# A windowed-attention and two-MLP kernel: the low-word shift of a 64-bit weight moved from VectorE to ScalarE

## The chip, the cores and the metric

The kernel runs on one core of a Trainium2 chip. The metric is the device time of one execution in microseconds; the time before is the median of three runs.

A core has five engines that run their own instruction queues side by side: TensorE (PE, with the weight load PEld beside it), VectorE (DVE), ScalarE (ACT), GpSimd (POOL) and SyncE (SP), which issues the DMAs here. Each engine executes its queue in order, and waits on semaphores of the others.

## The reference, cut to what matters

Three stages follow one another on a batch of 4 x 576 tokens, 8 heads of 64:

```python
x = downsampled_attention(q, k, v) + local_attention(q, k, v)   # window of +-3 positions
h = x @ w_in;  y = (h * cos(h)) @ w_out                         # 512 -> 2048 -> 512
out = ((y @ w_a) * (y @ w_b)) @ w_out2                          # 512 -> 1536 -> 512
```

The five weight matrices come as float64, since they are divided by a NumPy float64 scalar when they are drawn; q, k and v are float32. The chip's engines don't compute in float64, so the kernel turns every 64-bit weight into float32 by its bits: the high word holds sign, exponent and 20 bits of the mantissa, and the top three bits of the low word are the last three that a float32 keeps.

## The kernel before, in words

Weights come as 512 KB blocks, 128 x 512 values of two 32-bit words each, as the tile `raw` (first MLP) or `praw` (second MLP). `to_f32` (L102 to L110) converts a block in three instructions:

- L104, ACT: a Prelu over the high words, taken as float32, scales the exponent into place (in place, every second word).
- L106, DVE: the low words are shifted right by 29, which leaves the top three bits as an integer 0 to 7 (in place).
- L108, DVE: the high word shifted left by 3, OR the low word, gives the float32's bits.

There are 68 blocks. The first 32 belong to the first MLP (`w_in`, `w_out`): `wsplit` (L112 to L117) follows the conversion by an ACT copy to fp32r (`w`, L115) and a POOL subtraction that gives the rest (L116), so that a product of matrices is made of three fp32r products, `mm3` (L419 to L423: hi by hi, hi by lo, lo by hi). The other 36 belong to the second MLP: `pre_conv` (L587 to L603) converts them between the steps of the first MLP, forms sums on POOL (L600 to L603) or a split (ACT L596, POOL L597), and writes them to DRAM, from where the second MLP loads them.

The attention of 8 units of 288 tokens and the first MLP are interleaved. Unit 0 is computed first by itself, then a loop over `g` runs 112 steps: each step makes one block of 128 rows of `h` (`h_mm`), the cosine on ACT and DVE (`cos_a`, `cos_b`, L459 to L468), the split into `gh` (ACT L472) and `gl` (L476, on POOL for the first 8 steps and on DVE afterwards), and, three steps later, the product with `w_out` (`back_mm`). Pieces of the next unit's attention stand between (`unit_slots`): score tiles on DVE (L218 to L223), maxima (L236), an Identity with a per-partition bias on ACT (L237), softmax, transposes and the sums of v on POOL (`vd`, L173 to L175, fed by DMAs into `vs`). The first 32 conversions are asked for by `goal`: about two in a step for 8 steps, then about one in a step. All of them lie in the first 145 us. The last 36 conversions are spread over the time from 207 to 565 us. From 570 us on the second MLP runs alone, and no weight is converted there.

What stands ahead of what on an engine's queue isn't written out by hand alone: a scheduler lays the order down when the program is built, from the order of the source, the dependencies and its own estimates of durations. So the shifts of some blocks stand many steps ahead of the step that asks for them. Loads of raw blocks are paced: a load waits for the conversion (L108) of the block eight before it.

Of the kernel before, what the change touches and what calls it, by code (L numbers as in the profile page):

```python
# [9 lines left out]
F32 = mybir.dt.float32  # L10
# [3 lines left out]
U32 = mybir.dt.uint32  # L14
I64 = mybir.dt.int64
AF = mybir.ActivationFunctionType
ALU = mybir.AluOpType
# [41 lines left out]
def kernel(ctx, tc, qT, kT, vw, vds, w_in, w_out, w_a, w_b, w_out2, out):  # L59
    nc = tc.nc  # L60
    pe, act, dve, pool, sp = nc.tensor, nc.scalar, nc.vector, nc.gpsimd, nc.sync

    const = ctx.enter_context(tc.tile_pool(name="const", bufs=1))
# [28 lines left out]
    def after(ins, earlier):  # L92
        if earlier is not None:
            tc.add_manual_dep(ins.ins, earlier.name,
                              mybir.DependencyInfo(mybir.DependencyClass.NoSync, mybir.DependencyReason.DATA),
                              reason="paces the loads")
# [5 lines left out]
    def to_f32(raw, out=None, behind=None):  # L102
        lw, hh = raw[:, :, 0], raw[:, :, 1]
        ins = act.activation(out=hh.bitcast(F32), in_=hh.bitcast(F32), func=AF.Prelu, scale=2.0 ** -112, alpha=2.0 ** 32)  # L104
        after(ins, behind)
        ins = dve.tensor_scalar(out=lw, in0=lw, scalar1=29, scalar2=None, op0=ALU.logical_shift_right)  # L106
        after(ins, behind)
        ins = dve.scalar_tensor_tensor(out=lw if out is None else out, in0=hh, scalar=3, in1=lw, op0=ALU.logical_shift_left, op1=ALU.bitwise_or)  # L108
        marks.append(ins.ins)
        return lw  # L110

    def wsplit(raw, lo_eng):  # L112
        t = wp.tile([128, 2, 512], F32R, tag="w", name="w", bufs=33)
        lw = to_f32(raw)
        act.activation(out=t[:, 0], in_=lw.bitcast(F32), func=AF.Copy)  # L115
        lo_eng.tensor_tensor(out=t[:, 1], in0=lw.bitcast(F32), in1=t[:, 0].bitcast(F32), op=ALU.subtract)  # L116
        return t[:, 0], t[:, 1]  # L117
# [362 lines left out]
    for a in range(2):  # L480
        r = slice(64 * a, 64 * a + 64)
        pool.affine_select(out=mask[r], in_=mask[r], pattern=[[-1, W]], compare_op=ALU.is_ge,
                           fill=-8e9, base=3, channel_multiplier=1)
        pool.affine_select(out=mask[r], in_=mask[r], pattern=[[1, W]], compare_op=ALU.is_ge,
                           fill=-8e9, base=3, channel_multiplier=-1)

    if C["MK"]:
        identb = const.tile([128, 128], BF16, name="identb")
# [9 lines left out]
    if True:  # L498
# [88 lines left out]
        def pre_conv(n, g):  # L587
            nm, p, j = pre[n]
            t = praw[n]
            hh = t[:, :, 1]  # L590
            flat = t.rearrange("p f e -> p (f e)")
            fb = flat.bitcast(F32)
            k = len(marks)
            to_f32(t, flat[:, :512], h_ins[g])
            if nm == "2":
                act.activation(out=flat[:, 512:].bitcast(F32R), in_=fb[:, :512], func=AF.Copy)  # L596
                pool.tensor_tensor(out=flat[:, :512].bitcast(F32R), in0=fb[:, :512], in1=fb[:, 512:], op=ALU.subtract)  # L597
            else:
                a11, a12, a21, a22, s1, s2, s4 = (fb[:, 128 * i:128 * i + 128] for i in range(7))
                pool.tensor_tensor(out=s1, in0=a21, in1=a22, op=ALU.add)  # L600
                pool.tensor_tensor(out=s2, in0=s1, in1=a11, op=ALU.subtract)
                pool.tensor_tensor(out=a21, in0=a11, in1=a21, op=ALU.subtract)
                pool.tensor_tensor(out=s4, in0=a12, in1=s2, op=ALU.subtract)  # L603
# [113 lines left out]
        for g in range(NG + LAG):  # L717
            if g < NG:
                i, u, f = seq[g]
# [40 lines left out]
        for G in range(len(GROUPS)):  # L760
            for p in range(NP):
                prev = [("back", G, 0, p - 1, i, mh) for i in range(2) for mh in range(2)] if p else []
                a, b = ([("prod", G, p, nm, w) for w in ("P1", "P6", "P2", "P7", "P4", "P5", "P3")] for nm in "ab")
# [125 lines left out]
        for k, it in enumerate(items):  # L889
            stage(k + AH)  # L890
            if it[0] == "prod":
                product(k, *it[1:])
                if it[1] == 0:
                    fetch2(cv[0] + 1)
                    a, b = divmod(np_[0] - 4, 7)
# [3 lines left out]
            else:  # L899
                _, G, h, p, i, mh = it  # L900
                q = 2 * p + i
                if mh == 0 and (h == 1 or p == NP - 1):
                    r = q + 2 if h == 1 else i
                    if r < NF2:
                        f = r // 2 + NP * (r % 2)
# [66 lines left out]
```

## Time and profile before

| | us |
|---|---|
| median of 3 runs | 1010.39 (1010.36 to 1012.73) |
| the profiled execution, its own time | 1010.78 |
| its span, first to last instruction | 1009.0 |
| mean granted TensorE clock over the span | 0.983 |

A profile is one execution. Busy times of an engine are unions: two instructions that overlap in the engine's pipeline count once. Idle time of an engine only matters where it lies on the chain of work that ended last. The clock is the TensorE clock that was granted, as a share of 2.4 GHz.

### The profile page before, as it was taken

To read this page: it belongs to the slowest core of one execution; us is meant where nothing else is said; L and a number is where in the kernel's file an instruction comes from. 1 tells how busy PE (TensorE), PEld (TensorE's weight loads), DVE (VectorE), ACT (ScalarE), POOL (GpSimd) and SP (SyncE) were. 2 spreads that over 40 slices of the span, in tenths; PEclk is the share of its full clock that TensorE was granted. 3 is DMA by queue.
4 is the path that set the end of the run, shared out by engine and by line. 5 is a ranking of instruction groups with operands and counts; after the bars stand their busy time and mean duration, and the time that the engine had idled before them with its cause. 6 is when DMAs were issued, how large, how long until landed. Compare 5 with 4: busy or idle time off the path is not lost.

```text
span 1009.0 us, 18867 instructions
## 1 busy us (share of the span) xinstructions
PE 960.7 (95%) x6936; PEld 915.4 (91%) x6936; DVE 704.1 (70%) x1476; ACT 546.0 (54%) x1258; POOL 344.5 (34%) x463
## 2 busy tenths in 40 slices
PE   5878799999899999999998999999999999999998
PEld 3767789999798989899998999999999999999998
DVE  7788976587577877766466657676677667676751
ACT  4677757566485757566566643443444344434421
POOL 4878751005221341111046235433043330233310
PEclk9969999999899999999999999999999999999999
DMA  9644520153545463432277983316711128634000
GB/s 309 228 154 165 159 65 14 45 169 95 173 127 161 145 169 120 140 102 84 75 228 277 332 275 106 100 62 217 240 35 52 54 77 305 216 132 126 1 32 32
DMA packets 75644, 141.28 MB, mean 140 GB/s; under 512 B 6432, under 2 KB 46624, under 8 KB 75552
## 3 DMA queue, kind: packets, MB, share of 16 engines
q1 hardware_dynamic: 75552, 140.08, 42.2%
q8 instruction: 55, 0.90, 0.4%
q14 instruction: 37, 0.30, 0.1%
HBM read 110.95 MB, written 29.10 MB: 139 GB/s over the span
## 4 chain that ended last, share of the span: by engine, by line
PE 80%; DVE 6%; POOL 5%; DMA 4%; ACT 2%; issue 1%; SPq 1%; POOLq 0%; ACTq 0%; DVEq 0%
PE acc L420 10%; PE acc L421 10%; PE acc L422 10%; PE z L421 9%; PE z L422 9%; PE z L420 9%; PE h L420 6%; PE h L421 5%; PE h L422 5%; DMA vs<-in_vds_dram 2%; PE att L326 2%; PE att L207 1%; DVE raw L108 1%; PE att L319 1%; PE att L234 1%
## 5 line engine op out<-in xcount | busy, mean ns | idle before, releaser
L825 DVE TENSOR_TENSOR ev<-ev,z 128x384 f32<-128x384 f32 x252 | 135.4, 550 | 70.9 <-PE z L422 67.6
L420 PE MATMUL h<-xh,w 128*128 128x288 f32 (+1 forms) x448 | 147.6, 329 | 8.6 <-DVE gs L468 8.5
L420 PE MATMUL acc<-gh,w 128*128 128x288 f32 (+1 forms) x448 | 146.2, 326 | 3.9 <-DVE ev L453 3.9
L422 PE MATMUL h<-xh,w 128*128 128x288 f32 (+1 forms) x448 | 143.1, 319 | 2.2 <-POOL w L116 2.2
L421 PE MATMUL acc<-gl,w 128*128 128x288 f32 (+1 forms) x448 | 142.6, 318 | 2.4 <-POOL gl L476 2.4
L421 PE MATMUL h<-xl,w 128*128 128x288 f32 (+1 forms) x448 | 143.6, 321 | 0.0
L422 PE MATMUL acc<-gh,w 128*128 128x288 f32 (+1 forms) x448 | 141.6, 316 | 0.0
L783 POOL TENSOR_TENSOR sb<-w,sb 128x256 fp32r<-128x256 f32 x96 | 76.1, 794 | 185.9 <-ACT sb L781 140.1
L420 PEld LDWEIGHTS h<-xh,w 128*128 128x128 f32 x448 | 86.5, 193 | 15.3 <-DVE gs L468 12.1
L421 PE MATMUL z<-xl,sb 128*128 128x384 f32 x288 | 97.0, 337 | 0.0
L420 PE MATMUL acc<-gh,wb 128*128 128x384 f32 x288 | 96.9, 337 | 0.0
L422 PE MATMUL acc<-gh,wb 128*128 128x384 f32 x288 | 96.9, 337 | 0.0
L422 PE MATMUL z<-xh,sb 128*128 128x384 f32 x288 | 96.9, 336 | 0.0
L420 PE MATMUL z<-xh,sb 128*128 128x384 f32 x288 | 96.9, 336 | 0.0
L421 PE MATMUL acc<-gl,wb 128*128 128x384 f32 x288 | 96.9, 336 | 0.0
L781 ACT ACTIVATE sb<-w 128x256 fp32r<-128x256 f32 x144 | 59.9, 417 | 66.2 <-PE z L422 63.1
L420 PEld LDWEIGHTS acc<-gh,w 128*128 128x128 f32 x448 | 85.1, 190 | 10.6 <-DVE ev L453 5.0
L783 POOL TENSOR_TENSOR sb<-ws,sb 128x256 fp32r<-128x256 f32 x72 | 54.5, 757 | 108.6 <-ACT sb L781 84.8
L422 PEld LDWEIGHTS h<-xh,w 128*128 128x128 f32 x448 | 86.6, 193 | 4.5 <-POOL w L116 2.4
L421 PEld LDWEIGHTS acc<-gl,w 128*128 128x128 f32 x448 | 85.3, 191 | 4.2 <-POOL gl L476 2.7
L421 PEld LDWEIGHTS h<-xl,w 128*128 128x128 f32 x448 | 86.6, 193 | 1.6 <-issue 0.6
L422 PEld LDWEIGHTS acc<-gh,w 128*128 128x128 f32 x448 | 85.3, 190 | 1.4 <-issue 0.4
(135 smaller groups left out, 2280.4 us busy)
## 6 DMA issues: line engine op xcount, KB each, us to landing
wb<-wd SPq DMA_DIRECT2D x72, 512.0 KB
raw<-in_w_in_dram SPq DMA_DIRECT2D x16, 512.0 KB
raw<-in_w_out_dram SPq DMA_DIRECT2D x16, 512.0 KB
praw<-in_w_a_dram SPq DMA_DIRECT2D x12, 512.0 KB
praw<-in_w_b_dram SPq DMA_DIRECT2D x12, 512.0 KB
praw<-in_w_out_dram SPq DMA_DIRECT2D x12, 512.0 KB
wd<-praw SPq DMA_DIRECT2D x12, 512.0 KB
wd_a<-praw SPq DMA_DIRECT2D x12, 448.0 KB
```

The source lines that it names most:

```text
L108: ins = dve.scalar_tensor_tensor(out=lw if out is None else out, in0=hh, scalar=3, in1=lw, op0=ALU.logical_shift_left, op1=ALU.bitwise_or)
L207: pe.matmul(p[r, W * w:W * w + W], qt[u, hp][r, off:off + W], kt[b, hp][r, BASE[half] + off:BASE[half] + off + W], start=not pem, stop=True,)
L234: pe.matmul(p[a][:QD, :SD], qd[u, hp][r, :], kd[b, hp][r, :], start=True, stop=True)
L319: pe.matmul(p[64 * a:64 * a + 64, NB:NB + QD], vdt[b, hp][:, a, c], pd[u, hp][:, 2 * a + c], start=(c == 0), stop=(c == 1),)
L326: pe.matmul(p[64 * a:64 * a + 64, xo:xo + n], vt[u, hp // 2][r, w, a], pt[u, hp // 2][r, w, 64 * a + qo:64 * a + qo + n], start=True, stop ...
L420: i = pe.matmul(ps_out, lh, rh, start=start, stop=False)
L421: pe.matmul(ps_out, lh, rl, start=False, stop=False)
L422: pe.matmul(ps_out, ll, rh, start=False, stop=stop)
L781: act.activation(out=t[:, 0], in_=blk, func=AF.Copy)
L783: (dve if nst[0] % C["SD"] == 0 else pool).tensor_tensor(out=t[:, 1], in0=blk, in1=t[:, 0].bitcast(F32), op=ALU.subtract)
L825: dve.tensor_tensor(out=dst, in0=a, in1=z, op=ALU.add)
```

## The change

The DVE shift is replaced by an ACT Identity. It reads byte 3 of the low word (the top byte, an unsigned 8-bit integer, one in every 8 bytes), multiplies it by 1/32, adds a per-partition bias `down`, and writes the result as a 32-bit unsigned integer over the low word. The whole part of byte/32 is the same 0 to 7 that the shift gave. Whether the conversion to an integer rounds or cuts off is found out on the chip: 0.75 is converted once at the start; where this gives 1 the bias is -31/64, so that rounding leaves the whole part, and where it gives 0 the bias is 0. That adds a DVE memset, an ACT copy and a DVE multiplication on a 128 x 1 tile ahead of everything else. The dependencies of the two other instructions stay; the OR of L108 now waits for ACT alone.

```diff
         ins = act.activation(out=hh.bitcast(F32), in_=hh.bitcast(F32), func=AF.Prelu, scale=2.0 ** -112, alpha=2.0 ** 32)
         after(ins, behind)
-        ins = dve.tensor_scalar(out=lw, in0=lw, scalar1=29, scalar2=None, op0=ALU.logical_shift_right)
+        top = raw.rearrange("p f e -> p (f e)").bitcast(mybir.dt.uint8).rearrange("p (f b) -> p f b", b=8)[:, :, 3]
+        ins = act.activation(out=lw, in_=top, func=AF.Identity, scale=1.0 / 32.0, bias=down[:, :1])
         after(ins, behind)
         ins = dve.scalar_tensor_tensor(out=lw if out is None else out, in0=hh, scalar=3, in1=lw, op0=ALU.logical_shift_left, op1=ALU.bitwise_or)
...
+
+    down = const.tile([128, 1], F32, name="down")
+    near = const.tile([128, 1], U32, name="near")
+    dve.memset(down, 0.75)
+    act.activation(out=near, in_=down, func=AF.Copy)
+    dve.tensor_scalar(out=down, in0=near, scalar1=-31.0 / 64.0, scalar2=None, op0=ALU.mult)
```

## Rows read from the trace of the kernel before

**Rows 1.** The page: busy time, share and instruction count of each engine

```profile
PE 960.7 (95%) x6936; PEld 915.4 (91%) x6936; DVE 704.1 (70%) x1476; ACT 546.0 (54%) x1258; POOL 344.5 (34%) x463
```

**Rows 2.** By stretch: length; busy (count) PE, PEld, DVE, ACT, POOL; PEclk, DMA, GB/s

```profile
0.00:37.00 37.00, 23.77 (x238) 18.75 (x239) 26.39 (x67) 18.01 (x51) 21.48 (x40) 1.00 0.81 285
37.00:70.00 33.00, 25.04 (x234) 19.46 (x233) 31.48 (x68) 24.51 (x62) 23.67 (x23) 0.84 0.53 182
70.00:115.00 45.00, 38.41 (x288) 36.33 (x287) 38.11 (x56) 34.28 (x80) 34.27 (x30) 0.89 0.55 184
115.00:145.00 30.00, 26.45 (x239) 24.01 (x238) 24.81 (x47) 18.86 (x44) 20.71 (x25) 0.94 0.18 55
...
207.00:540.00 333.00, 327.42 (x2781) 303.14 (x2778) 234.01 (x562) 215.74 (x488) 91.56 (x150) 0.99 0.46 144
540.00:570.00 30.00, 26.82 (x130) 25.27 (x129) 23.24 (x38) 19.59 (x39) 14.57 (x21) 0.94 0.76 248
```

**Rows 3.** Chain that ended last, shares by line: 37-70, 70-115 and 115-145 us

```profile
by line: DVE raw L106 14.2%; DVE raw L108 10.6%; PE att L326 7.3%; DVE smx L223 6.8%; PE att L207 6.1%; DVE smd L293 5.4%; DVE sl L275 4.7%; PE att L319 4.3%; DVE mxd L236 4.0%; DVE smx L218 3.9%; ACT L464 3.9%; DVE mx L222 3.6%; PE h L421 
...
by line: DVE raw L108 24.7%; DVE raw L106 12.4%; PE h L420 7.1%; DVE gl L476 6.7%; PE h L422 6.2%; PE h L421 6.1%; ACT w L115 5.3%; PE att L326 3.7%; ACT raw L104 2.8%; POOL w L116 2.7%; DVE gs L468 2.6%; DVE gs L460 2.4%; issue 2.4%; PE at
...
by line: POOL w L116 23.9%; DMA vs<-in_vds_dram 23.7%; issue 11.8%; POOL vd L174 10.7%; POOL vd L173 9.9%; POOL vd L175 9.6%; ACT w L115 6.8%; ACT smd L237 1.8%; DVE gs L468 1.6%; ACT gh L472 1.5%; ACT gs L467 1.1%; ACT gs L464 1.1%; DVE gl
```

**Rows 4.** L106 by tile: min/median/max ns, first and last start

```profile
L106 DVE TENSOR_SCALAR raw<-raw x32: 399/667/1549, 6.4 to 117.9; 128x512 uint32<-128x512 uint32 x32
...
L106 DVE TENSOR_SCALAR praw<-praw x36: 404/422/1003, 216.8 to 562.4; 128x512 uint32<-128x512 uint32 x36
```

**Rows 5.** L106 alone by stretch: DVE busy time (count)

```profile
37.00:70.00 33.00, 6.51 (x9) 0.84 0.53 182
70.00:115.00 45.00, 11.69 (x14) 0.89 0.55 184
...
207.00:540.00 333.00, 14.79 (x31) 0.99 0.46 144
```

**Rows 6.** Timeline around 55 us: start, duration, engine, line, operation

```profile
54.31 1.28 DVE L108 SCALAR_TENSOR_TENSOR raw<-raw 128x512 uint32<-128x512 uint32 x2
...
54.63 3.49 POOL L476 TENSOR_TENSOR gl<-gs,gh 128x288 fp32r<-128x288 f32 x1 [1.75 <-ACT gh L472]
...
55.51 0.75 DVE L106 TENSOR_SCALAR raw<-raw 128x512 uint32<-128x512 uint32 x2
```

**Rows 7.** ACT groups by form: busy us, mean ns; idle before, releaser

```profile
L104 ACT ACTIVATE praw<-praw 128x512 f32<-128x512 f32 x36 | 23.9, 664 | 4.9 <-DMA praw<-in_w_out_dram 4.9
L237 ACT ACTIVATE smd<-att,mxd 72x144 f32<-72x144 f32 x64 | 22.5, 370 | 19.3 <-DVE mxd L236 19.1
...
L311 ACT COPY smd<-att 72x288 f32<-72x288 f32 x32 | 12.4, 389 | 2.3 <-PE att L309 1.2 <-DVE sd L288 1.0
...
L596 ACT ACTIVATE praw<-praw 128x512 fp32r<-128x512 f32 x12 | 7.6, 631 | 0.8 <-DVE praw L108 0.4
...
L336 ACT COPY up<-att 128x72 f32<-128x72 f32 x32 | 6.9, 216 | 15.3 <-PE att L326 15.1
```

**Rows 8.** ACT timeline at 107 us, two Prelu conversions back to back

```profile
107.44 1.23 ACT L104 ACTIVATE raw<-raw 128x512 f32<-128x512 f32 x2
```

**Rows 9.** L104 alone by stretch: ACT busy time (count)

```profile
37.00:70.00 33.00, 2.89 (x5) 0.84 0.53 182
70.00:115.00 45.00, 9.39 (x14) 0.89 0.55 184
...
207.00:540.00 333.00, 20.58 (x31) 0.99 0.46 144
```

**Rows 10.** Waits of TensorE in 207-540 us: total, times, longest

```profile
PE att L207 <- ACT praw L596: 3.8, 1, 3.8
```

**Rows 11.** ACT timeline of the first 7 us

```profile
0.73 1.28 ACT L237 ACT_TABLE_LOAD   x1 [0.73 <-PEq L958]
6.50 0.38 ACT L237 ACTIVATE smd<-att,mxd 72x144 f32<-72x144 f32 x1 [4.48 <-DVE mxd L236]
```

## The prediction

> **What bounds the kernel now.** I read the page's busy times first: TensorE is busy 95% of the span, DVE 70%, ACT 54% [rows 1]. That is an average, so the next view is the table by stretch, cut where conversions begin and end [rows 2]. From 207 to 540 us TensorE is busy 327.4 of 333 us: only 5.6 us are there to be won. From 37 to 145 us, where the first 32 weight blocks are converted, TensorE is busy 25.0 of 33, 38.4 of 45 and 26.4 of 30 us, so 18 us are idle, and the granted clock is 0.84, 0.89 and 0.94. If the missing shares are stretches at the lower of the two levels, 1.2 GHz, they mean another 33 x 0.16 = 5.3, 45 x 0.11 = 5.0 and 30 x 0.06 = 1.8 us of clock. In the stretch from 37 to 70 us DVE is busy 31.5 of 33 us: it is the bound. From 70 to 115 us TensorE and DVE stand at 38.4 and 38.1, and ACT and POOL at 34.3 each.
>
> The third view is the chain that ended last in the same stretches [rows 3]. From 37 to 70 us the shift L106 leads it with 14.2% (4.7 us); from 70 to 115 us the OR L108 leads with 24.7% and L106 follows with 12.4% (5.6 us). From 115 to 145 us the chain is POOL's subtraction of weights and the v sums with their DMAs; L106 doesn't show.
>
> **What is removed.** 68 shifts leave DVE. Undisturbed one takes 0.40 us, the least of both tiles; the first 32 have a median of 0.667 and go up to 1.549, the last 36 a median of 0.422 [rows 4]. By stretch that is 6.5 us in 37 to 70 (9 shifts), 11.7 in 70 to 115 (14), and 14.8 in 207 to 540 (31) [rows 5]. What is above 0.40 is not work. Around 55 us two ORs, two shifts and further ORs run on DVE without a gap, and a POOL subtraction over 288 columns that began among them takes 3.49 us [rows 6]: the two engines hold each other up when both work from SBUF. Such a hold goes to the next DVE instruction when the shift is gone, so I count a shift as 0.40 us, and its full time as the far end: 3.6 to 6.5 us in 37 to 70, 5.6 to 11.7 in 70 to 115.
>
> **What is added.** 68 Identities on ACT. No row shows one that reads bytes. The nearest is the Prelu L104 on the same blocks with the same stride of 8 bytes, 0.664 us; a copy of the same length that lies dense takes 0.631 (L596) [rows 7], so the stride matters little. The bias from a tile has its price: L237, an Identity with such a bias over 144 columns from PSUM, takes 0.370 us, while copies from PSUM without one take 0.216 over 72 columns and 0.389 over 288 [rows 7], which puts 144 at 0.274. That is 0.096 more, so I take 0.664 + 0.096 = 0.76 us; the ends are 0.63 (dense, no bias) and twice L104, 1.33. Back to back, two L104 take 1.23 us [rows 8], so the second adds 0.57; an Identity then adds 0.57 + 0.10 = 0.67 us to ACT (ends 0.53 and 1.24).
>
> The Trainium skill (ScalarE: Activation LUTs, What ACT_TABLE_LOAD costs) gives 280 ns plus 0.833 ns an element for an activation with such a bias, 0.71 us for 512 columns. By that figure the tight stretch below would have 14 x 0.05 = 0.7 us less on ACT; the sum goes by the rows.
>
> As many Identities as Prelu operations fall in a stretch, so the counts are those of L104: 5, 14 and 31 [rows 9]. ACT's busy time becomes 24.5 + 5 x 0.67 = 27.9 of 33 us, and 34.3 + 14 x 0.67 = 43.7 of 45 us, while DVE falls to 31.5 - 3.6 = 27.9 and 38.1 - 5.6 = 32.5. So the first stretch is relieved and in the second ACT takes over DVE's place.
>
> **The new wait.** L108 waits for ACT alone now. On ACT's queue the Identity stands ahead of the weight copy L115 and of the cosine's and split's operations (L459 to L472); DVE's L460 and L468, POOL's L116 and, three steps later, TensorE wait for those.
>
> **The start.** The three setup operations go ahead of ACT's and DVE's first work. ACT loads its table at 0.73 us and then sits idle 4.48 us before its first operation at 6.50 [rows 11]; that idle time hides one copy, and even one more table load of 1.28 us. Without that cover it would cost at most 1.5 us. The dependency of the bias on DVE is long met when the first Identity needs it. No DMA is added, and the queues of SP and POOL lose nothing and gain nothing.
>
> **The sum, stretch by stretch.**
> - 0 to 37 us: POOL's sums of v wait for DMAs here; one hold of POOL by a shift goes. I take -0.4 (ends 0 and -1.5).
> - 37 to 70 us: 9 x 0.40 = 3.6 us of DVE's work leave a stretch that DVE bounds; one Identity in five I let fall on the chain, 0.67. That is -2.9 (ends: the chain's whole share of L106, -4.7, and all five Identities on the chain with nothing won, +3.4).
> - 70 to 115 us: 5.6 us leave DVE, 9.4 come to ACT, which still fits in 45 us with 1.3 to spare. I take 0 (ends -5.6 and +6.4, the latter worked out below).
> - 115 to 145 us: the chain is POOL's and the DMAs'. 0 (ends -1 and +2).
> - 207 to 540 us: 31 x 0.67 = 21 us come to ACT, which goes from 215.7 to 236.5 of 333 us, and 31 x 0.40 = 12 us leave DVE. TensorE's work hides both. Only where TensorE waits behind the conversions of a block already, 3.8 us once [rows 10], do I add one Identity: +0.7 (ends 0 and +3). If that cover is gone, an Identity ahead of the cosine costs 0.67 each time.
> - 540 to 570 us: five conversions, shift against Identity: 0 (ends -0.6 and +2).
> - Clock: with about a third of the idle time in 37 to 70 us gone, I take back a fifth of its 5.3 us: -1.1 (ends 0 and -2.6).
>
> Together -0.4 - 2.9 + 0 + 0 + 0.7 + 0 - 1.1 = -3.7 us against the profiled execution's 1010.78, or 1007.1. That execution lies 0.39 above the median of the runs, so the forecast is 1006.7 against 1010.39.
>
> **The rivals.**
> - *The large gain.* All of L106's share of the chain goes, 4.7 + 5.6 = 10.3 us, and half of the first stretch's clock comes back, 2.6: 1010.39 - 12.9 = 997.5. For it: DVE saturated in the first stretch. Against it: ACT at 43.7 of 45 us in the second.
> - *Hidden.* The holds between POOL and DVE pass to L108, whose place on the chain is the larger, and ACT's new work eats what is left: 1010, between 1008 and 1012. For it: L108 with 24.7% of the chain stands right behind the shift.
> - *ACT becomes the bound.* From 70 to 115 us the busiest engine got 38.4 of 45 us, 85%. If ACT gets no more either, its 43.7 us need 51.4: +6.4; with two Identities ahead of TensorE's waits in 207 to 540 us, +1.3, and nothing won before 70 us: 1018.1. It decides if ACT keeps more than 1.3 us of idle time in the 45. For it: the copy, the cosine and the split share ACT's queue with the conversion; against it: POOL and DVE, on which ACT waits, are freed. The Trainium skill (ScalarE: Activation LUTs, Rules for kernel authors) speaks for this side: simple arithmetic belongs on VectorE, which is faster for each element. Here a shift has 0.40 us at best on DVE, and the nearest ACT operation 0.664 [rows 4, 7], so by that rule the time would be this rival's, 1018.
> - *It doesn't do what it says.* Each Identity calls for a table load of 1.28 us. L237 is an Identity too, 64 times [rows 7], and the load at 0.73 us is the only one on its line [rows 11]. I give it 0.02.
>
> **How the numbers follow.** 0.3% of 1010.39 is 3.0 us, about what can be told from no change here. The forecast has 0.43, with a range of its own from 1003.5 to 1009; some 0.28 of it lies below 1007.4 and 0.15 above. The large gain has 0.15, hidden 0.18, ACT as the bound 0.22 and the table loads 0.02; these two end slower, but for 0.03 of the first, which stays within 0.3%. So faster 0.28 + 0.15 = 0.43, same 0.15 + 0.18 + 0.03 = 0.36, slower 0.21. The order on the queues is laid down anew when durations change, which no row shows; I let it widen the range to 997 to 1017, which leaves out about a third of the large gain and half of the slow cases, under 0.2.
>
> **What would show it.** Right: from 37 to 70 us DVE is no longer full and TensorE's idle time falls from 8 us to about 5; an Identity takes about 0.76 us; ACT is the busiest engine for the weights after 70 us; the time past 145 us is unchanged to within 1 us. Wrong: ACT idle more than 1.3 us in that stretch with TensorE waiting for the cosine or for weights; Identities far above 0.76 us; L108 longer than before by what the shift gave up; or a wait for ACT at TensorE in 207 to 540 us that sums to more than 3 us.

## The result and the profile after

The changed kernel takes 1001.69 us (median of four runs, 999.70 to 1003.24) against 1010.79 us (1010.36 to 1012.73) for the kernel before; the ratio is 0.988 with a 95% interval of 0.985 to 0.991. It is 1.2% faster, 9.1 us between the medians, more than twice the forecast of 3.7 us. The profiled execution took 1003.24 us, 7.5 less than that of before, with a span of 1001.5 us.

The busy times of the page after, to be laid beside [rows 1]:

```profile
PE 964.9 (96%) x6936; PEld 917.0 (92%) x6936; DVE 669.1 (67%) x1410; ACT 581.9 (58%) x1327; POOL 327.9 (33%) x463
```

DVE has 35.0 us less, ACT 35.9 more, POOL 16.6 less, though the change gives POOL nothing to do or to leave. The table by stretch, cut as in [rows 2] (columns: stretch, length, busy time and count of PE, PEld, DVE, ACT and POOL, PEclk, DMA share, GB/s):

```profile
0.00:37.00 37.00, 22.62 (x238) 17.88 (x239) 22.98 (x61) 20.39 (x55) 19.14 (x39) 0.71 0.84 285
37.00:70.00 33.00, 31.30 (x175) 24.50 (x175) 22.31 (x51) 22.67 (x56) 16.39 (x19) 0.55 0.45 150
70.00:115.00 45.00, 39.88 (x393) 37.08 (x393) 32.15 (x58) 41.74 (x95) 32.49 (x34) 0.92 0.57 179
115.00:145.00 30.00, 28.69 (x223) 26.78 (x223) 21.35 (x43) 26.86 (x65) 17.80 (x24) 1.00 0.36 123
145.00:207.00 62.00, 59.32 (x572) 54.95 (x571) 41.85 (x99) 40.13 (x95) 10.73 (x10) 1.00 0.19 58
207.00:540.00 333.00, 325.68 (x2765) 300.65 (x2764) 224.91 (x528) 233.41 (x521) 90.05 (x155) 1.00 0.46 143
540.00:570.00 30.00, 29.43 (x142) 28.09 (x143) 17.49 (x30) 22.13 (x42) 10.39 (x15) 0.94 0.85 288
```

From 70 to 115 us DVE falls from 38.1 to 32.2 and ACT rises from 34.3 to 41.7, much as forecast, and yet TensorE is busier than before, 39.9 for 38.4, and in the 30 us after that 28.7 for 26.4. ACT has 3.3 us of idle time in the 45, not the 1.3 of the forecast, for the work that falls into a stretch isn't the same. A fixed stretch of time is a poor ruler when the work moves; a fixed piece of work is a better one. I take the steps `g` of the first MLP, and as a step's mark the first ACT operation of the cosine, of which there are 112, one a step. Step 4 and step 20, first before and then after (the timeline of ACT: start, duration, line, operation):

```profile
74.56 0.41 ACT L459 ACTIVATE gs<-h 128x288 int32<-128x288 f32 x1 [0.56 <-PE h L422]
...
152.03 0.39 ACT L459 ACTIVATE gs<-h 128x288 int32<-128x288 f32 x1
```

```profile
77.35 0.41 ACT L460 ACTIVATE gs<-h 128x288 int32<-128x288 f32 x1
...
146.32 0.40 ACT L460 ACTIVATE gs<-h 128x288 int32<-128x288 f32 x1
```

From step 4 to step 20 the kernel before takes 77.5 us, the changed one 69.0: 8.5 us are won there, where the blocks from about the 14th on are converted. The same piece of work in the columns of the table above, before and then after:

```profile
74.56:152.03 77.47, 64.98 (x533) 60.23 (x531) 65.54 (x108) 53.78 (x124) 52.58 (x53) 0.94 0.39 127
```

```profile
77.35:146.32 68.97, 63.02 (x541) 58.72 (x539) 49.26 (x92) 62.99 (x142) 46.30 (x52) 0.98 0.49 161
```

DVE has 16.3 us less to do in it and ACT 9.2 more; ACT is now as busy there as TensorE. From step 20 to the end another 1.8 us are won (855.2 for 857.0). Up to step 4 the changed execution is 2.8 us late, and its clock was low there, as its table in tens shows:

```profile
10.00:20.00 10.00, 5.57 (x59) 3.86 (x55) 9.58 (x26) 7.82 (x20) 2.14 (x5) 0.77 0.88 248
20.00:30.00 10.00, 6.93 (x69) 5.47 (x70) 7.75 (x24) 4.77 (x19) 9.29 (x14) 0.50 1.02 357
...
50.00:60.00 10.00, 10.00 (x48) 6.92 (x49) 3.54 (x11) 6.40 (x15) 4.34 (x6) 0.50 0.73 241
60.00:70.00 10.00, 8.30 (x40) 7.80 (x41) 9.93 (x24) 8.75 (x26) 5.00 (x4) 0.67 0.23 92
```

From about 15 to past 60 us TensorE was granted 0.50, the lower of its levels, after it had been busy 3.6 us of the first ten; the kernel before, with 4.2 there and 5.7 in the next ten, was granted 1.00 and had its low between 60 and 77 us. Not every execution of the changed kernel has it: another one, profiled later (run e12 below), had a mean clock of 0.991 in place of 0.969 and a span of 994.6 us, with step 4 at 73.3 and step 20 at 142.1 us. A low clock need not cost that time: e1's execution below was granted 0.50 from 15 to 46 us and reached step 4 at 73.5.

The parts that were priced one by one:

```profile
L107 ACT ACTIVATE praw<-praw,down 128x512 uint32<-128x512 uint8 x36 | 27.1, 753 | 0.0
L107 ACT ACTIVATE raw<-raw,down 128x512 uint32<-128x512 uint8 x32 | 24.2, 757 | 0.1
...
L104 ACT ACTIVATE raw<-raw 128x512 f32<-128x512 f32 x32 | 21.5, 673 | 0.7 <-DMA raw<-in_w_in_dram 0.7
```

An Identity takes 757 and 753 ns; 0.76 us had been taken. At the start (timeline of ACT) the table load and the one copy stand in idle time, and the first real operation comes 0.07 us later than before:

```profile
0.73 1.28 ACT L491 ACT_TABLE_LOAD   x1 [0.73 <-PEq L965]
2.02 0.20 ACT L491 ACTIVATE near<-down 128x1 uint32<-128x1 f32 x1
6.57 0.38 ACT L238 ACTIVATE smd<-att,mxd 72x144 f32<-72x144 f32 x1 [4.34 <-DVE mxd L237]
```

What came unforeseen is the OR, here before and then after (groups of DVE by form: count, busy us, mean ns, idle before, releaser):

```profile
L108 DVE SCALAR_TENSOR_TENSOR raw<-raw 128x512 uint32<-128x512 uint32 x32 | 31.1, 983 | 1.5 <-ACT raw L104 1.3
```

```profile
L109 DVE SCALAR_TENSOR_TENSOR raw<-raw 128x512 uint32<-128x512 uint32 x32 | 26.1, 819 | 9.4 <-ACT raw L107 9.2
```

The OR itself, untouched by the change, went from 983 to 819 ns. The missing shift alone doesn't explain that: in e4 below, which has no shift either, the OR takes 984 ns. With the shift (24.6 us for the first 32, the mean of 783 ns that the group has) DVE spent 55.7 us on these blocks and now spends 26.1: 29.6 us have gone, more than the far end of the forecast, which was the shift's full time. Elsewhere DVE lost some of it again: three other groups grew by 7.5 us together (by the line numbers of the kernel before: L293 from 16.1 to 19.5, L476 over 288 columns from 39.0 to 41.4, L223 from 17.7 to 19.4).

In 207 to 540 us the 3.8 us that TensorE waited behind a conversion [rows 10] are gone; the longest waits there in this execution are:

```profile
PE h L421 <- DVE gs L469: 1.4, 3, 0.7
PE att L208 <- DVE smx L219: 1.2, 1, 1.2
```

### The profile page after: what moved, and what is told of

Its sections match the earlier page's. It is cut to its first block, busy times and chain, and to the rows that moved or that the text cites. A ratio compares the mean times of both kernels' runs of the same rounds, so it can differ in the third digit from the quotient of the medians.

```text
span 1001.5 us, 18883 instructions
## 1 busy us (share of the span) xinstructions
PE 964.9 (96%) x6936; PEld 917.0 (92%) x6936; DVE 669.1 (67%) x1410; ACT 581.9 (58%) x1327; POOL 327.9 (33%) x463
## 5 line engine op out<-in xcount | busy, mean ns | idle before, releaser
L423 PE MATMUL acc<-gh,w 128*128 128x288 f32 (+1 forms) x448 | 142.1, 317 | 0.0
L421 PEld LDWEIGHTS acc<-gh,w 128*128 128x128 f32 x448 | 84.8, 190 | 9.1 <-issue 2.9
L469 DVE SCALAR_TENSOR_TENSOR gs<-gs,h 128x288 f32<-128x288 f32 (+1 forms) x112 | 55.2, 493 | 56.6 <-ACT gs L468 56.3
```

The source lines that it names most:

```text
L421: i = pe.matmul(ps_out, lh, rh, start=start, stop=False)
L423: pe.matmul(ps_out, ll, rh, start=False, stop=stop)
L469: dve.scalar_tensor_tensor(out=s, in0=s, scalar=1.0, in1=hps[g], op0=ALU.subtract, op1=ALU.mult, reverse0=True)
```

## The experiments

Twelve runs were made, each timed against the kernel before. The ratios are from all executions. Steps 4 and 20 are from the one that was profiled, and one execution can differ from the next by some us: the two of the changed kernel are 4 us apart at step 4, and e7's is the slowest of its ten (1011.6 us, median 1007.35).

| run | shift of blocks 1-13, 14-32, last 36 | ratio to before, 95% interval | step 4, us | step 20, us | 4 to 20 |
|---|---|---|---|---|---|
| before | DVE, DVE, DVE | | 74.6 | 152.0 | 77.5 |
| e3, setup alone | DVE, DVE, DVE | 0.9988 (0.9969 to 1.0008) | 80.0 | 153.2 | 73.2 |
| e9, shift in two pieces | DVE, DVE, DVE | 0.9988 (0.9968 to 1.0009) | 78.0 | 153.3 | 75.2 |
| e2, last 36 | DVE, DVE, ACT | 0.9962 (0.9944 to 0.9980) | 81.5 | 155.3 | 73.8 |
| e10, early 13 | ACT, DVE, DVE | 0.9996 (0.9973 to 1.0018) | 74.1 | 151.7 | 77.6 |
| e7, late 19 | DVE, ACT, DVE | 0.9940 (0.9912 to 0.9968) | 81.1 | 151.1 | 70.0 |
| e1, first 32 | ACT, ACT, DVE | 0.9866 (0.9842 to 0.9891) | 73.5 | 142.6 | 69.1 |
| changed kernel | ACT, ACT, ACT | 0.9880 (0.9854 to 0.9906) | 77.3 | 146.3 | 69.0 |
| e12, changed again | ACT, ACT, ACT | 0.9881 (0.9845 to 0.9916) | 73.3 | 142.1 | 68.8 |
| e8, constant bias | ACT, ACT, ACT | 0.9879 (0.9837 to 0.9920) | 74.9 | 144.7 | 69.7 |
| e11, constant bias | ACT, ACT, DVE | 0.9938 (0.9914 to 0.9961) | 74.4 | 145.1 | 70.7 |
| e4, no low word | none | 0.9887 (0.9851 to 0.9922) | 74.4 | 146.2 | 71.8 |
| e5, extra held operation | ACT and DVE, ACT and DVE, ACT | 0.9960 (0.9940 to 0.9980) | 79.5 | 151.2 | 71.7 |
| e6, extra free operation | ACT, ACT, ACT | 0.9896 (0.9846 to 0.9946) | 75.2 | 145.2 | 70.0 |

The edits are shortened. Those of e1, e2, e5, e6 and e8 are shown against the changed kernel, those of e4 and e9 against the kernel before, those of e7 and e10 against e1.

**Which blocks carry it: e1, e2, and the order by itself: e3.**

```diff
-        ins = act.activation(out=lw, in_=top, func=AF.Identity, scale=1.0 / 32.0, bias=down[:, :1])
+        if out is None:    # e1; e2 has "is not None"
+            ins = act.activation(out=lw, in_=top, func=AF.Identity, scale=1.0 / 32.0, bias=down[:, :1])
+        else:
+            ins = dve.tensor_scalar(out=lw, in0=lw, scalar1=29, scalar2=None, op0=ALU.logical_shift_right)
```

e3 is the kernel before with the five lines of the setup and nothing else.

> Identity on ACT for the 32 blocks of the first MLP only; the other 36 keep the shift on DVE. If the gain is DVE relieved while the first 32 blocks are converted (theory A), this keeps nearly all of it: 0.989 to 0.994 of before, about 1002 us. If the gain comes from the queues being laid down in another order (theory B), the time has no reason to stand near either kernel: anything from 0.985 to 1.005. If it came from the last 36 blocks, 0.998 to 1.002.

> Identity on ACT for the last 36 blocks only; the first 32 keep the shift. Theory A: only the one wait of TensorE near 262 us can go, so 0.996 to 1.001 of before, 1006 to 1011 us. Theory B: anything from 0.985 to 1.005. If the last 36 carry the gain: 0.990 or less.

> The shift stays on DVE for all 68 blocks; only the three setup operations are added and their result is not used. Theory A: 0.998 to 1.002 of before. Theory B: the order on the queues changes here too, so a move of several us, 0.3% or more to either side, speaks for it.

e1 keeps the whole gain, e2 has a third of it, and e3 none. Theory A (the gain is DVE relieved while the first 32 blocks are converted) holds against theory B (another order on the queues): the first 32 blocks carry the gain, and the other order that e3 has doesn't bring it. The last 36 have their own small share: in e1, where they keep the shift, TensorE's wait behind a block's conversion (at 262 us in the kernel before, at 254 in e1) is there as in [rows 10] (waits of TensorE in 207 to 540 us):

```profile
PE h L420 <- DVE gs L468: 4.1, 3, 3.4
PE att L207 <- ACT praw L596: 3.7, 1, 3.7
```

The second line is gone in the changed kernel and in e12. Between step 34 and step 46 the kernels with Identity for these blocks gain 3.6 to 4.4 us on the kernel before (e12: 201.6 to 256.2, before: 210.7 to 268.9, so 3.6), and e1 gains 0.4. Much of it is lost again later: from step 46 to the last step e2 takes 314.5 us and the kernel before 311.1. e2 ends with 0.4%.

**Is ACT's work hidden: e4.** The low word is left out of the weights altogether; the OR takes zeros.

```diff
-        ins = dve.tensor_scalar(out=lw, in0=lw, scalar1=29, scalar2=None, op0=ALU.logical_shift_right)
-        after(ins, behind)
-        ins = dve.scalar_tensor_tensor(..., in0=hh, scalar=3, in1=lw, ...)
+        ins = dve.scalar_tensor_tensor(..., in0=hh, scalar=3, in1=zero[:, :1].to_broadcast([128, 512]), ...)
```

> Leaves out the low word altogether: neither shift nor Identity, the OR takes a zero from a 128 x 1 tile, so a float32 weight lacks its last three mantissa bits. Neither DVE nor ACT has the work. Theory A: at least as fast as the changed kernel, 0.980 to 0.988 of before, 990 to 999 us, since ACT is relieved too; if the 0.76 us of the Identity is wholly hidden on ACT, the same as the changed kernel, 0.988. Theory B: again anything, also slower than the changed kernel.

The same as the changed kernel. In the tight stretches ACT has 4 and 8 us less than in the changed kernel, and TensorE gets no more:

```profile
70.00:115.00 45.00, 39.54 (x312) 36.87 (x309) 33.33 (x48) 37.54 (x87) 35.29 (x33) 0.95 0.61 202
115.00:145.00 30.00, 26.45 (x237) 23.78 (x236) 24.22 (x48) 18.66 (x46) 18.09 (x24) 0.94 0.24 70
```

That doesn't yet show that the Identity is free, for e4 changes the OR too. With `zero` as its second operand the OR of the first 32 blocks is as long as in the kernel before, and POOL is busy 338.1 us against 327.9 in the changed kernel:

```profile
L108 DVE SCALAR_TENSOR_TENSOR raw<-raw,zero 128x512 uint32<-128x512 uint32 x32 | 31.2, 984 | 7.3 <-ACT raw L104 6.8
```

What ACT gave may have gone there. e8 below takes a smaller piece from ACT and leaves the OR's operands alone.

**DVE's time or its holding: e5, e6.** Both are the changed kernel with one more DVE operation on the dead high words of the first 32 blocks, after the OR, whose result nobody reads.

```diff
         marks.append(ins.ins)
+        if out is None:
+            dve.tensor_scalar(out=hh, in0=hh, scalar1=29, scalar2=None, op0=ALU.logical_shift_right)            # e5
+            dve.tensor_reduce(out=hh[:, :1].bitcast(F32), in_=hh[:, :248].bitcast(F32), axis=AX.X, op=ALU.max)  # e6, in its place
```

> The changed kernel, with one more shift of 128 x 512 words on DVE for each of the first 32 blocks, after the OR, on the dead high words, whose result nobody reads: DVE has the time back (0.40 us undisturbed, as the shift removed), ACT keeps the Identity. If DVE's time is what was won (theory A), most of the gain goes: 0.995 to 1.005 of before. If the gain was that the OR and what follows no longer stand behind the shift, as a matter of dependency and not of DVE's time (rival), it stays near 0.988.

> As the run with the extra shift, but the extra DVE operation is a maximum over 248 columns of the dead words, about 0.40 us, of a kind that the trace shows with no lengthening while POOL works (the sums of L180 take 0.44 and 0.74 us throughout). The queues are the same on PE, POOL and SP as with the extra shift. If DVE's own 0.40 us is the price (A1): the same as with the extra shift within 0.3%. If the shift's price is that it and POOL hold each other up (A2): this one is faster than the extra shift by 0.4% or more, 0.988 to 0.993 of before.

The extra operation of e5 in its views by tile (min/median/max) and by form (count, busy us, mean ns):

```profile
L109 DVE TENSOR_SCALAR raw<-raw x32: 411/420/1840, 20.6 to 168.2; 128x512 uint32<-128x512 uint32 x32
```

```profile
L109 DVE TENSOR_SCALAR raw<-raw 128x512 uint32<-128x512 uint32 x32 | 19.5, 608 | 0.2
```

The same for e6:

```profile
L109 DVE TENSOR_REDUCE raw<-raw x32: 393/401/416, 20.5 to 162.1; 128x1 f32<-128x248 f32 x32
```

```profile
L109 DVE TENSOR_REDUCE raw<-raw 128x1 f32<-128x248 f32 x32 | 12.9, 402 | 0.2
```

Both take 0.40 to 0.42 us undisturbed. The maximum never takes more than 0.416 and costs next to nothing, 0.9896 against 0.9880, well inside the intervals. The shift goes up to 1.84 us, has a mean of 0.608, and gives back two thirds of the gain.

The pair is close. In the two traces the queues of TensorE and POOL have the same order, and those of DVE and ACT differ by a few neighbours that change places between 107 and 114 us. Step 4 comes well before that, and 4.3 of the 7.5 us between the two executions are there already (the medians are 6.2 apart): with the same order, an extra operation of the same undisturbed length costs more when it is the shift. The busy times of the two pages, e5 and then e6:

```profile
PE 963.5 (96%) x6936; PEld 914.9 (91%) x6936; DVE 686.5 (68%) x1442; ACT 584.0 (58%) x1327; POOL 335.1 (33%) x463
```

```profile
PE 959.6 (96%) x6936; PEld 913.1 (91%) x6936; DVE 682.0 (68%) x1442; ACT 582.7 (58%) x1327; POOL 328.8 (33%) x463
```

DVE is busy 4.5 us longer with the shift and POOL 6.3 us longer, though POOL's 463 instructions are the same: the hold lengthens both engines. Up to step 4 it is POOL alone, 45.0 us against 41.5, with DVE at 53.8 and 53.9 and a mean clock of 0.89 and 0.91. So the loss there isn't DVE's own time, and the subtraction of 3.49 us among DVE's shifts and ORs [rows 6] fits. Which of POOL's operations carries the loss to TensorE wasn't traced. The rival of a pure dependency falls: nothing depends on the extra shift.

**Early or late: e7, e10.**

```diff
-        if out is None:
+        if out is None and len(marks) >= 13:    # e7; e10 has "< 13"
```

> Identity for the blocks 14 to 32 of the first MLP only (those converted after about 70 us in the trace of before); the first 13 and the last 36 keep the shift. If the gain arises while ACT, DVE and POOL convert one or two blocks in each step after 70 us, as the two traces show, this keeps it: 0.986 to 0.991 of before. If it arises before 70 us, where my prediction put it, 0.996 to 1.001.

> Identity for the first 13 blocks only (converted before about 70 us); the other 55 keep the shift. The counterpart of the run with blocks 14 to 32, which kept half of the gain. If the halves add up: 0.991 to 0.995 of before. If what is won before 70 us is lost at the next bound: 0.997 to 1.002, and then the run with blocks 14 to 32 fell short by its start alone.

The halves don't add up, 0.994 and 1.000 against 0.987 for both, and the columns of steps 4 and 20 suggest why. With late blocks on ACT, step 20 follows step 4 by 68.8 to 70.7 us, in all seven kernels that have it without an extra shift. With late blocks on DVE step 20 comes between 151.7 and 155.3 us in all five, however early step 4 was (74.1 to 81.5). So before, the start is waited away: my reading is that DVE with its shifts can't have the late blocks ready sooner. Blocks 1 to 13 bear on when step 4 comes: 73.3 to 75.2 us with Identity, Copy or no low word, 77.3 in the one with the long low clock, 78.0 to 81.5 with shifts or with e5's extra shift, except for the kernel before itself, with 74.6. Part of that spread may be the clock, though e1 came at 73.5 with a mean of 0.70: up to step 4 its mean was 0.83 or 0.84 in e2, e7 and e9, 0.90 in the kernel before and e3, 0.91 in e10 and e12. In its profiled execution e7 has the fast run from step 4 on but begins it at 81.1, and e10 begins at 74.1 and is held up after that. By the ratios both are needed for all of the gain.

**Meant as a shift that POOL can't hold up: e9.**

```diff
-        ins = dve.tensor_scalar(out=lw, in0=lw, scalar1=29, scalar2=None, op0=ALU.logical_shift_right)
+        cut = 511 if out is None else 512
+        ins = dve.tensor_scalar(out=lw[:, :cut], in0=lw[:, :cut], scalar1=29, ...)
+        if out is None: after(dve.tensor_scalar(out=lw[:, cut:], in0=lw[:, cut:], scalar1=29, ...), behind)
```

> The kernel before, with the shift of the first 32 blocks on DVE in two pieces, 511 words and one word. The Trainium skill (VectorE: DVE Perf Modes, What auto-detection actually checks) has an operation with one SBUF source run at two elements a cycle only where the length is even or the same on both sides; no run here has shown that yet. If the piece of 511 then takes more than 0.5 us, and no longer stretches while POOL works, the holding goes and DVE's own time rises, to some 0.65 to 0.75 us a block. If the holding alone is the price of the shift: 0.988 to 0.994 of before. If DVE's whole time is, held or not: 0.997 to 1.003, since 0.7 us stands against a mean of 0.78 before. If the length changes nothing: 1.000 to 1.005, one more operation.

```profile
L106 DVE TENSOR_SCALAR raw<-raw x32: 404/614/3229, 6.7 to 121.8; 128x511 uint32<-128x511 uint32 x32
...
L107 DVE TENSOR_SCALAR raw<-raw x32: 122/141/147, 7.0 to 125.2; 128x1 uint32<-128x1 uint32 x32
L109 DVE SCALAR_TENSOR_TENSOR raw<-raw x32: 676/868/2198, 8.4 to 140.7; 128x512 uint32<-128x512 uint32 x32
```

The piece of 511 words still takes 0.404 us at the least and is held up to 3.2 us. The test was badly chosen: the length was odd but the same on both sides. For that the Trainium skill (VectorE: DVE Perf Modes, What auto-detection actually checks) still gives two elements a cycle, and the run agrees with it, 0.404 us for 511 words against 0.399 for 512 [rows 4]. A shift on DVE that isn't held has not been tried. What is left is that one more DVE operation of 0.14 us a block, 4.5 us in all, cost nothing that can be measured.

**Cheaper on ACT: e8, e11, e12.** In e8 a Copy with the constant bias -31/64 takes the place of the Identity with the bias tile, and the setup goes; e11 does so for the first 32 blocks and leaves the last 36 on DVE; e12 is the changed kernel again. The constant takes for granted that the conversion to an integer rounds, which no time here can show.

```diff
-        ins = act.activation(out=lw, in_=top, func=AF.Identity, scale=1.0 / 32.0, bias=down[:, :1])
+        ins = act.activation(out=lw, in_=top, func=AF.Copy, scale=1.0 / 32.0, bias=-31.0 / 64.0)
```

> The changed kernel with the bias -31/64 as a constant of a Copy, without the setup operations and the bias tile: each conversion 0.66 to 0.67 us in place of 0.76, 0.09 x 32 = 3 us less on ACT in the first 145 us. If ACT bounds that stretch now: 0.984 to 0.987 of before. If ACT's time is hidden, as leaving out the low word suggests: 0.987 to 0.990, the same as the changed kernel.

> The two cheapest parts together: a Copy with the constant bias for the first 32 blocks, the shift on DVE for the last 36, no setup. If ACT has slack wherever it converts, the same as the changed kernel within 0.3%: 0.985 to 0.990 of before. If ACT's 0.76 us in the first 145 us or the 21 us in 207 to 540 us cost anything: 0.980 to 0.985.

> The changed kernel again, on the same chip as the run with the two cheapest parts, so that the two can be compared: 0.986 to 0.991 of before.

The Copy has a median of 672 ns for the 757 of the Identity (e8, by tile):

```profile
L106 ACT ACTIVATE raw<-raw x32: 650/672/753, 7.6 to 151.9; 128x512 uint32<-128x512 uint8 x32
```

The 0.085 us a block, 2.7 us for the first 32, are worth nothing that can be measured. e11 was expected beside e1 and e8 and is 0.6 to 0.7% behind them, with the interval of e1 clear of its own. Up to step 20 it is within 0.4 us of e8; then it loses, 2.9 us by step 34. Its stretches from 145 us on, and after them those of e1:

```profile
145.00:207.00 62.00, 58.38 (x547) 54.91 (x546) 38.92 (x93) 37.11 (x89) 9.56 (x9) 0.94 0.17 53
207.00:540.00 333.00, 328.02 (x2778) 304.10 (x2777) 233.89 (x559) 215.58 (x487) 93.77 (x152) 0.99 0.45 143
```

```profile
145.00:207.00 62.00, 59.85 (x577) 55.36 (x577) 41.57 (x102) 38.94 (x95) 8.52 (x8) 1.00 0.21 66
207.00:540.00 333.00, 323.57 (x2741) 299.68 (x2741) 233.32 (x555) 215.47 (x485) 97.13 (x159) 0.99 0.45 142
```

From 145 to 207 us e11 has a clock of 0.94, which stood at 0.83 from 150 to 170 us; e1's is 1.00. TensorE had been busy 8.6 and 8.5 of 10 us in the two slices before; in e8, which kept 1.00, it had been busy 7.7 and 8.2, so these shares don't explain it. And from 207 us on it keeps the wait that the shift for the last 36 leaves:

```profile
PE att L207 <- ACT gs L467: 3.8, 1, 3.8
```

e11 differs from e1 in the Copy, the setup and the order that the scheduler laid down with them. That the order is what cost the 0.6% and brought on the clock is likely, but wasn't shown; the cause stays open. No version beat the changed kernel clear of the intervals: e1, e8 and e12 are all within 0.2% of it.

## Why the prediction was right, and where its sum was off

The direction, the range (997 to 1017) and the price of the parts held: an Identity 0.76 us, the start for nothing, ACT nearly full after 70 us. That the time fell inside the range is in part luck: the range had been widened for a new order on the queues, and the gain came from a stretch that the sum had at 0. The size was off, 3.7 us forecast against 9.1 between the medians, and it was off in named terms.

- *0 to 37 us, -0.4, and 37 to 70 us, -2.9.* Step 4 comes 2.8 us later in the profiled execution and 1.3 us earlier in e12. The place was wrong: DVE was full there, and Identity for those blocks alone (e10) wins nothing by the end.
- *70 to 115 us, 0, and 115 to 145 us, 0.* This is the term that was mis-sized. From step 4 to step 20 the gain is 8.5 us. The step that failed is "ACT takes over DVE's place". ACT did come to 41.7 of 45 us, busier than DVE had been with 38.1, and to 63.0 of 69.0 us from step 4 to step 20, but the work went through faster all the same: an engine's busy share by itself doesn't make it the bound. How near ACT is to being the next one is open: e8 took 2.7 us from it and won nothing, and e4, which took more, lengthened the OR.
- *"Such a hold goes to the next DVE instruction, so I count a shift as 0.40 us."* This was one of two ends, and the truth lay between them: by the pages DVE has 35.0 us less, where 68 x 0.40 us would have been 27.2 and the shifts' full time was 24.6 + 18.2 = 42.8. So about half of the hold passed on. It didn't go to the OR of the first 32 blocks, which lost 0.16 us, but to other DVE operations. What the sum had nowhere is the other side, POOL's 16.6 us. The pair e5 and e6 shows that the 0.40 us are nearly free and that the holding is the price.
- *207 to 540 us, +0.7.* Steps 34 to 46 won 3.6 to 4.4 us where the last 36 blocks had Identity or Copy, and the time from step 20 to the end, which was to stay within 1 us after 145 us, fell by 1.8 us and in e12 by 4.5. An Identity behind the Prelu was expected to lengthen TensorE's wait at 262 us; the wait went. Why the new order avoids it I didn't test.
- *Clock, -1.1.* The profiled execution had 0.71 and 0.55 up to 70 us, worse than before, and won all the same. No run took the clock by itself, so its term stays open. e12's stretches are those of the same kernel with a clock near that of before:

```profile
37.00:70.00 33.00, 28.88 (x230) 23.26 (x230) 24.01 (x55) 25.40 (x64) 19.09 (x21) 0.84 0.44 151
70.00:115.00 45.00, 40.38 (x358) 38.11 (x357) 31.05 (x56) 40.92 (x92) 32.02 (x34) 0.93 0.60 195
115.00:145.00 30.00, 28.37 (x219) 26.18 (x218) 21.69 (x42) 27.41 (x64) 16.60 (x20) 1.00 0.30 98
```

Of the rivals, the large gain (997.5) put its sum in the chain's share of L106 and came a little nearer (4.2 us off, the forecast 5.0): the chain had named the right instruction. That ACT becomes the bound was to be decided by its idle time from 70 to 115 us, more or less than 1.3 us: it kept 3.3, and the kernel got faster. "Hidden", 1008 to 1012, falls with the time, and no table load stands on the Identity's line. The rule of the Trainium skill (ScalarE: Activation LUTs, Rules for kernel authors), by which such arithmetic belongs on VectorE because it is faster there for each element, would have lost 1.2% here: per element it is right, 0.40 us against 0.76, but the price of the shift was mainly what POOL and DVE did to each other.

## What to carry to other kernels

Price a DVE operation by what it does beside POOL, not by its undisturbed time: the spread between the least and the largest duration of its group says whether it is one that gets held, and moving such an operation to an engine with idle time can pay even if it takes twice as long there. Compare two traces at the same step of the work, not at the same microsecond. An early win that is waited away later is no win; look for the step at which all variants arrive at about the same time. And look at what an experiment changes beside what it is meant to change: e4 freed ACT, and made the OR longer.

## What the runs showed that was not expected

- Two DVE operations of the same undisturbed length, 0.40 us, in the same place: a shift of 128 x 512 words reaches 1.84 us in e5 (3.2 us in e9), a maximum over 248 columns never leaves 0.393 to 0.416 us in e6.
- POOL's busy time fell by 16.6 us over the span in the changed kernel and rose by 6.3 from e6 to e5, with the same 463 instructions: the holding goes both ways. It isn't the shift alone: e4, without a shift, has 338.1 us, 6.4 below the kernel before.
- ACT reads single bytes 8 apart and writes words 8 apart in 0.672 us for 512 elements with a constant bias, as fast as the Prelu on whole words (0.673 in the changed kernel); the bias from a tile adds 0.09 us.
- With ratios that agree to 0.2% between e1, e8, e12 and the changed kernel, e11, made of parts of them, is 0.6% slower. Parts that are each free need not be so together; the order that comes with them is the likely reason, not a shown one.
